# A fused attention and Fourier-mixing kernel: the first head pair folded too, 32 more score scans in the front, and the loop's cross products spread over 32 more steps

## The chip, the cores and the metric

The kernel runs on one core of one Trainium2 chip. The metric is device time in microseconds of one execution; the median of the runs shown is taken. In this text TensorE is PE in the profile's rows (its weight loads PEld), VectorE is DVE, ScalarE is ACT, GpSimd is POOL, and SyncE, which issues most of the transfers, is SP.

## The reference

For one sequence of 2048 rows of width 512, a gate mixes two results:

```python
g = sigmoid((x * gate_w).sum(-1, keepdims=True))
qkv = x @ wqkv                                   # 32 heads of width 16
a = softmax(q @ k^T * 16**-0.5) @ v @ wo         # per head, then the output projection
b = dft_seq_re @ (x @ dft_hid_re^T) - dft_seq_im @ (x @ dft_hid_im^T)
out = g * a + (1 - g) * b
```

All of it is in single precision. The weights of the attention are 64 times as large as is usual, so that the softmax needs the maximum of each row of scores subtracted.

## The kernel before, in words

The 32 heads are worked as 16 pairs. A float32 operand is split into a high and a low part, and a product is three matmuls (high by high, high by low, low by high). Most matmuls have at most 64 rows of the array and run as two side by side, each 512 columns wide; such a side-by-side couple is called a **slot** below (`halves_of` issues one, line 204).

**Scans.** Before a pair's exponentials can be taken, the maximum of each row of its scores must be known. A *scan* (there are 64 for a pair, 1024 in all) computes 128 query rows against 512 keys for both heads of the pair, one slot of TensorE work. A *plain* scan (`scan`, line 154) leaves the maximum to one VectorE reduction over 1024 numbers. A *folded* scan (`scan_folded`, line 173) works on key blocks two and two: the even block holds the difference of the keys of two blocks, ScalarE takes its positive part into the tile `fold` (line 177), and VectorE adds the odd block's scores and takes the maximum (line 179). That needs *key differences* in DRAM (`kf_d`), next to the plain keys (`k_d`).

**The front**, the first 655 us, is a sequence of products written out by hand: projections of q and k (`project_t`, 32 tiles of 12 slots), of v and the two hidden-side Fourier products (`project_s`, 48 tiles of 12 slots), and then most of the sequence-side Fourier product (22 tiles of 48 slots). Each product slot calls `beside`, which puts a scan between them at the spacing that `scan_at` sets (`PACE`, `SUMS`, `BESIDE`, `PART`, `SWAP`: so many product slots to a scan), until `FRONT` scans are done. Small steps are queued with `after(n, ...)`, n product slots ahead; each engine takes its steps in the order in which they were issued. In the kernel before, the 64 scans of pair 0 are plain and the other 644 of the front are folded. The key differences of pairs 4 to 7 are made when their keys are projected (`difference`), those of pairs 0 to 3 and 8 to 11 later, by `fold_keys`, which reads keys back from DRAM.

**The loop** has 512 steps, 32 for each pair. A step multiplies q by 128 keys for 1024 queries of both heads (line 229: one slot into a two-bank tile, `qk_both`, and one slot into two single banks, `qk_single`), takes the exponentials on ScalarE (line 253, 1024 columns, tile `eb`; line 261, twice 512 columns, tiles `e`), and multiplies the exponentials of an earlier step by v (line 775, tile `pvb`). Up to step `MIX` a step also has one plain scan. From `MIX` on the scans are done, and each step takes one piece of `fill`: first 32 steps of the sequence-side Fourier product (`spectral`), then the seven *cross products* (`crosses`, 14 tiles of 24 slots, as 8 pieces of 3 slots each), and from step `OUT` on the output projection (`mix_heads`, 9 slots a tile, in two pieces of 4 and 5 slots or four pieces of 2, 2, 2 and 3, and then `mix_some`). From `MIX` on the products with v of two steps are issued together in the even step:

```python
for _ in range(min(len(pend), 1) if step < MIX else 0 if step % 2 else 2):
    done = flush()
```

An even step's piece of `fill` is issued ahead of its products of q and k, an odd step's behind them, so the two pieces of an odd step and the even step behind it stand next to each other on TensorE. `qk_both` has one two-bank tile, which the next step needs again; `qk_single` takes its two banks out of three in turn (`bank`), so that one of the two was used in the step before.

Of the kernel before, what the change touches and what calls it, by code (L numbers as in the profile page):

```python
# [18 lines left out]
P = 128  # L19
# [17 lines left out]
SAVED = 2 * CROSS  # L37
# [5 lines left out]
PART_PAIR, END_PAIR = PARTS  # L43
SEQ = [(p, i) for p in EARLY for i in range(SCANS)]
SEQ += [(p, i) for p, n in PARTS.items() for i in range(n)]
SEQ += [(p, i) for p in (PART_PAIR, 12, 13, 14, 15, END_PAIR) for i in range(PARTS.get(p, 0), SCANS)]
ROWS = {SCANS * n + (20 if n else 40): p for n, p in enumerate(EARLY[1:])}
ROWS.update({SCANS * len(EARLY) - 60: PART_PAIR, SCANS * len(EARLY) - 34: END_PAIR})
NWARM = 20
MIX = TOTAL - FRONT + 1  # L50
OUT = MIX + NB * LATER - SAVED
HALVED = MIX + NB * (LATER - CROSS)
SLOW = 3
# [13 lines left out]
def build(tc, xT, wqkv, wo, wrT, wiT, cr, ci, ct, gate, out):  # L67
    nc = tc.nc
    with ExitStack() as ctx:
# [112 lines left out]
        def shift(p, copy=nc.vector.tensor_copy, sub=nc.vector.tensor_sub):  # L182
# [10 lines left out]
            of = mx[p].rearrange("p j b c -> p (j b) c")[:, :, 0:2 if p in EARLY[1:] else 4]  # L193
# [76 lines left out]
        with ExitStack() as pf:  # L270
# [36 lines left out]
            def beside():  # L307
# [6 lines left out]
                while seen[0] < FRONT and pace[1] >= 1.0:  # L314
                    pace[1] -= 1.0
                    n = seen[0]
                    if n == FOLDED.start:
# [20 lines left out]
            def behind(n):  # L338
                if n in FOLDED:
                    scan_folded(n, 1, *beds)  # L340
                    return n
# [49 lines left out]
            def begin_folds():  # L391
# [4 lines left out]
                scan_at(BESIDE)  # L396

            with ExitStack() as px:
# [28 lines left out]
                def fold_keys(f, g):  # L427
# [3 lines left out]
                    parts = [(a, b)]  # L431
                    if f:
                        for i, v in enumerate((a, b)):
                            nc.sync.dma_start(v, ks_d[f][:, (c + i) * 512:(c + i + 1) * 512])
                    else:

                        parts.append([rp.tile([P, 512], F32, tag="raw", name="fl") for _ in range(2)])
                        for n in range(2):
                            for i in range(2):
                                nc.sync.dma_start(parts[n][i], k_d[f][:, n, (c + i) * 512:(c + i + 1) * 512])  # L440
                        nc.sync.dma_start(kf_d[f][:, :, (c + 1) * 512:(c + 2) * 512],
                                          k_d[f][:, :, (c + 1) * 512:(c + 2) * 512])
# [6 lines left out]
                    wait = 0 if f else 26  # L449
                    after(14 + wait // 2, nc.gpsimd.tensor_sub, a, a, b)  # L450
                    if wait:
                        after(33, nc.gpsimd.tensor_sub, parts[1][0], *parts[1])
                        after(39, nc.gpsimd.tensor_add, a, a, parts[1][0])
                    after(wait + 22, nc.scalar.copy, hi, a)
                    after(wait + 24, nc.gpsimd.tensor_sub, lo, a, hi.bitcast(F32))
                    after(wait + 28, store, 0, hi)
                    after(wait + 31, store, 1, lo)
# [3 lines left out]
                def difference(f, c, s):  # L461
# [6 lines left out]
                    hi = ep.tile([P, 512], F32R, tag="gb", name="dh", bufs=1)  # L468
                    lo = a.bitcast(F32R)
# [10 lines left out]
                def project_t(w, dst, f, c, ps=None):  # L480
# [5 lines left out]
                    s = ep.tile([P, 512], F32, tag="ty", name="s", bufs=3)  # L486
# [3 lines left out]
                    on_vector = pace[0] in (None, SUMS)  # L490
                    if on_vector:
                        after(5, nc.vector.tensor_add, s, ps[1], tx)
                    else:
                        after(3, nc.scalar.copy, s, ps[1])
                        after(5, nc.gpsimd.tensor_add, s, s, tx)
                    late = 0 if on_vector else 6

                    def store(i, v):
                        nc.sync.dma_start(dst[f][:, i, c * 512:(c + 1) * 512], v.bitcast(F32))
                        if folded and f and c % 2:  # L500
# [6 lines left out]
                    after(9 + late, nc.scalar.copy, hi, s)  # L507
                    after(10 + late + late // 3, nc.gpsimd.tensor_sub, lo, s, hi.bitcast(F32))
                    after(14 + late, store, 0, hi)
                    after(20 + late, store, 1, lo)  # L510
# [72 lines left out]
                order += [(w, dst, 0, c) for c in range(1, NC) for w, dst in ((wq, q_d), (wk, k_d))]  # L583
# [22 lines left out]

                for t in range(NB):
# [22 lines left out]
                for n, wait in enumerate((18, 78, 138, 202)):  # L630
                    after(wait, fold_keys, 2 * (n // 2), n % 2)
# [20 lines left out]
            with ExitStack() as py:  # L652
# [36 lines left out]
                for n, (ph, t, u) in enumerate(coef):  # L689
# [6 lines left out]
                    if n == len(coef) - 2 * NU:  # L696
# [632 lines left out]
```

## Time and profile before

| what | value |
|---|---|
| median of 3 runs (lowest, highest) | 1714.47 us (1714.12 to 1715.61) |
| the profiled execution's own time | 1715.43 us |
| its span in the profile | 1713.6 us |
| TensorE clock granted | 0.999 |
| busy: PE, PEld, DVE, ACT, POOL | 99%, 60%, 69%, 87%, 45% |
| first scan of the front; first exponentials of the loop | 58 us; 658.5 us |
| loop, first to last tile `eb` | 658.5 to 1695.9 us, 512 of them |

A row of a group of instructions has the source line, the engine, the operation, the tiles written and read, the shapes and a count, then busy time and the mean of one, then the idle time ahead of them and what ended it. A row of the timeline has its start, its length, and the instructions merged into it. Matmuls are pipelined and their ends are modelled, so that a busy TensorE says little by itself; counts of matmuls in a stretch and start times say more.

### The profile page before, as it was taken

How to read it: one execution, taken by the hardware profiler on the slowest of the kernel's cores; microseconds unless marked ns; L12 is line 12 of the kernel's file. 1: busy time of each engine (PE TensorE's matmuls, PEld its weight loads, DVE VectorE, ACT ScalarE, POOL GpSimd, SP SyncE). 2: the span in 40 equal slices, each digit the busy share in tenths (PEclk: the TensorE clock that was granted, in tenths of full speed). 3: DMA queues.
4: the chain of work that ended last, by engine and by line, in shares of the span. 5: the costliest groups of instructions: out<-in, count | busy, mean ns of one | idle time of the engine just before them, and what ended most of it. 6: DMA issues, size and time to landing. Idle time of an engine off the chain costs nothing.

```text
span 1713.6 us, 36496 instructions
## 1 busy us (share of the span) xinstructions
PE 1700.1 (99%) x13560; PEld 1033.2 (60%) x13560; DVE 1189.9 (69%) x2179; ACT 1496.6 (87%) x2472; POOL 764.1 (45%) x909
## 2 busy tenths in 40 slices
PE   9999999999999999999999999999999999999998
PEld 6888888989888895333333333333345555555554
DVE  5798888889899996666666676666642455654343
ACT  6447889888888888999999999999998988888876
POOL 3583335755555762433535455353422333334222
PEclk9999999999999999999999999999999999999999
DMA  7783457533337665356544445453436465576733
GB/s 255 237 286 86 149 153 224 155 107 108 112 106 199 176 132 109 89 128 149 138 112 113 121 114 135 100 124 85 95 73 144 133 148 148 141 160 168 192 93 126
DMA packets 148962, 240.97 MB, mean 141 GB/s; under 512 B 50048, under 2 KB 60784, under 8 KB 142192
## 3 DMA queue, kind: packets, MB, share of 16 engines
q1 hardware_dynamic: 133520, 217.27, 47.5%
q0 software_dynamic: 14688, 20.33, 5.0%
q8 instruction: 106, 1.74, 0.5%
q10 hardware_dynamic: 576, 1.05, 0.2%
q14 instruction: 72, 0.59, 0.1%
HBM read 158.34 MB, written 81.01 MB: 140 GB/s over the span
## 4 chain that ended last, share of the span: by engine, by line
PE 95%; issue 1%; POOL 1%; DMA 1%; DVE 1%; ACT 0%; SPq 0%; DVEq 0%; POOLq 0%; ACTq 0%
PE pvb L775 29%; PE xy L204 24%; PE s L229 19%; PE s L173 9%; PE s L204 9%; PE s L154 5%; POOL el L297 1%; DMA raws<-wqkv 0%; DMA qs<-q_d 0%; DVE y L890 0%; DVE fold L179 0%; ACT fold L177 0%; DVE s L297 0%; SPq L543 0%; SPq L542 0%
## 5 line engine op out<-in xcount | busy, mean ns | idle before, releaser
L253 ACT ACTIVATE eb<-s 128x1024 f32<-128x1024 f32 x512 | 582.0, 1137 | 59.6 <-PE s L229 59.5
L261 ACT ACTIVATE e<-s 128x512 f32<-128x512 f32 x1022 | 612.3, 715 | 0.0
L156 DVE TENSOR_REDUCE mx<-s 128x2 f32<-128x1024 f32 x380 | 461.0, 1224 | 197.5 <-PE s L154 197.3
L775 PE MATMUL pvb<-eb,va 128*17 128x512 f32 x2052 | 514.6, 597 | 0.0
L775 PE MATMUL pvb<-e,va 128*17 128x512 f32 x2044 | 513.6, 597 | 0.0
L179 DVE CUSTOM_DVE_ANT_0 fold<-s,fold 128x512 f32<-128x512 f32 x644 | 433.2, 690 | 57.3 <-PE s L173 29.9
L177 ACT ACTIVATE fold<-s 128x512 f32<-128x512 f32 x644 | 381.4, 603 | 76.8 <-PE s L173 58.9
L229 PEld LDWEIGHTS s<-qs,ks 50*128 50x128 f32 x2048 | 215.4, 185 | 361.4 <-ACT eb L253 269.4
L229 PE MATMUL s<-qs,ks 50*128 50x512 f32 x2048 | 424.3, 435 | 0.0
L204 PE MATMUL xy<-b,c 64*128 64x512 f32 x2448 | 394.7, 392 | 0.2 <-ACT c L352 0.2
L173 PE MATMUL s<-ks,qs 48*128 48x512 f32 x1288 | 306.1, 403 | 1.7 <-DVE mx L179 0.9
L204 PEld LDWEIGHTS xy<-b,c 64*128 64x128 f32 x2448 | 285.7, 187 | 16.9 <-issue 1.0
L173 PEld LDWEIGHTS s<-ks,qs 48*128 48x128 f32 x1288 | 167.1, 184 | 40.4 <-DVE mx L179 10.7
L775 PEld LDWEIGHTS pvb<-eb,va 128*17 128x17 f32 x2052 | 70.0, 96 | 188.1 <-issue 178.5
L154 PE MATMUL s<-ks,qs 48*128 48x512 f32 x760 | 158.5, 394 | 0.9 <-DMA qs<-q_d 0.9
L204 PE MATMUL s<-b,b 64*128 64x512 f32 x1050 | 136.3, 391 | 0.0
L794 POOL DMA_DIRECT2D r_d<-lc x31 | 18.0, 580 | 260.6 <-DVE lc L793 212.9
L204 PE MATMUL xy<-w,b 64*128 64x512 f32 x768 | 114.8, 392 | 0.0
L204 PEld LDWEIGHTS s<-b,b 64*128 64x128 f32 x1050 | 100.3, 185 | 23.4 <-issue 1.0
L787 POOL DMA_DIRECT2D lc<-ob x124 | 63.0, 515 | 114.4 <-DVE ob L784 109.6
L384 POOL TENSOR_TENSOR c<-craw,c 128x512 fp32r<-128x512 f32 x84 | 110.2, 1312 | 6.7
L796 POOL DMA_DIRECT2D rb<-r_d x124 | 60.5, 494 | 110.6 <-DMA r_d<-lc 104.7
(148 smaller groups left out, 1567.3 us busy)
## 6 DMA issues: line engine op xcount, KB each, us to landing
qs<-q_d SPq DMA_DIRECT2D x68, 256.0 KB
craw<-cr SPq DMA_DIRECT2D x60, 256.0 KB
craw<-ct SPq DMA_DIRECT2D x48, 256.0 KB
ks<-k_d SPq DMA_DIRECT2D x46, 256.0 KB
kept_None<-sum SPq DMA_DIRECT2D x40, 256.0 KB
craw<-kept_None SPq DMA_DIRECT2D x40, 256.0 KB
qs<-q_d SPq DMA_DIRECT2D x68, 128.0 KB
craw<-ci SPq DMA_DIRECT2D x32, 256.0 KB
```

The costliest lines, as they stand in the source:

```text
L154: nc.tensor.matmul(ps[:, j, :], qs[b:b + 48, qb * P:(qb + 1) * P], ks[b:b + 48, c * 512:(c + 1) * 512], start=True, stop=True)
L156: nc.vector.tensor_reduce(mx[p][:, :, qb, c], ps, axis=AX.X, op=ALU.max)
L173: nc.tensor.matmul(ps, qs[b:b + 48, qb * P:(qb + 1) * P], ks[b:b + 48, c * 512:(c + 1) * 512], start=True, stop=True)
L177: nc.scalar.activation(fold[j], ps, AF.Relu)
L179: nc.vector.tensor_tensor_reduce(out=fold[j], in0=ps, in1=fold[j], scale=1.0, scalar=-3.0e38, op0=ALU.add, op1=ALU.max, accum_out=mx[p][:, ...
L204: nc.tensor.matmul(ps[j], lhs[r], rhs[r], start=first, stop=last)
L229: nc.tensor.matmul(pss[j], ks[b:b + 50, kb * P:(kb + 1) * P], qs[b:b + 50, q0:q0 + 512], start=True, stop=True)
L253: nc.scalar.activation(e, ps, AF.Exp, scale=SCALE)
L261: nc.scalar.activation(e[j], pss[j], AF.Exp, scale=SCALE)
L384: sub(lo, raw, hi.bitcast(F32))
L775: nc.tensor.matmul(pvb[r:r + VC, :], va[:, kb, 2 * p + j, :], es[c][j], start=kb == 0, stop=kb == NB - 1, tile_position=(0, r))
L787: nc.gpsimd.dma_start(lc[32 * n:32 * n + 32, :], ob[r + DH:r + VC, :].rearrange("p (s e) -> p s e", e=16))
```

## The change

- Pair 0 is folded like the others. Its key differences, and those of pairs 1 to 3, are made in the prologue by `difference`, from the sums while they are still in SBUF; the projections of k are issued ahead of those of q in the first row group for that. `fold_keys` now serves pairs 8 to 11 and 12 to 15.
- The front has 740 scans in place of 708, all folded: the pairs in order 0 to 10 whole, 16 of pair 12 and 20 of pair 11. The spacing is narrower in the projections of q and k (2.95 and 3.6 for 3.9 and 5.2 product slots to a scan) and a little narrower in the last part (2.11 for 2.15). The sum of the two halves of a projection is always taken on VectorE now.
- `MIX` goes from step 317 to 285. The cross products of a tile are cut into 10 pieces (3, 2, 2, 3, 2, 2, 3, 2, 2, 3 slots) in place of 8 pieces of 3, so they take 140 steps in place of 112. `OUT` goes from 461 to 457, and five tiles of the output projection in place of three are cut into four pieces.

```diff
-FRONT = 564 + 16 * LATER - SAVED
-FOLDED = range(SCANS, FRONT)
-PACE, SUMS, BESIDE, PART, SWAP = 3.9, 5.2, 2.72, 2.15, 2.97
-EARLY = [0, 4, 5, 6, 7, 1, 2, 3, 8, 9]
-PARTS = {10: 20, 11: FRONT - SCANS * len(EARLY) - 20}
+EARLY = range(11)
+PARTS = {12: 16, 11: 20}
+FRONT = SCANS * len(EARLY) + sum(PARTS.values())
+PACE, SUMS, BESIDE, PART, SWAP = 2.95, 3.6, 2.72, 2.11, 2.97
...
-OUT = MIX + NB * LATER - SAVED
 HALVED = MIX + NB * (LATER - CROSS)
-SLOW = 3
+STEPS = [3, 2, 2, 3, 2, 2, 3, 2, 2, 3]
+TURN = 2 * len(STEPS)
+OUT = HALVED + 7 * TURN
+SLOW = 5
...
-                scanned[p], loads = row_loads(p, nc.sync, kf_d if p else k_d)
+                scanned[p], loads = row_loads(p, nc.sync, kf_d)
...
-                    if n not in FOLDED:
-                        scan(n, s1())
-                        done = n
-                    else:
-                        scan_folded(n, 0, *beds)
-                        done = behind(n - 1)
+                    scan_folded(n, 0, *beds)
+                    done = behind(n - 1)
...
-                    hi = ep.tile([P, 512], F32R, tag="gb", name="dh", bufs=1)
-                    lo = a.bitcast(F32R)
+                    hi = (ep.tile([P, 512], F32R, tag="gb", name="dh", bufs=1) if f else
+                          rp.tile([P, 512], F32R, tag="raw", name="dh"))
+                    lo = b.bitcast(F32R)
...
-                    on_vector = pace[0] in (None, SUMS)
-                    if on_vector:
-                        after(5, nc.vector.tensor_add, s, ps[1], tx)
-                    else:
-                        after(3, nc.scalar.copy, s, ps[1])
-                        after(5, nc.gpsimd.tensor_add, s, s, tx)
+                    after(5, nc.vector.tensor_add, s, ps[1], tx)
...
-                    if folded and f == 1:
+                    if folded and f < 2:
                         difference(f, c, s)
-                    if folded and f == 2:
+                    if folded and f > 1:
                         after(10, nc.sync.dma_start, ks_d[f][:, c * 512:(c + 1) * 512], s)
...
-                order += [(w, dst, 0, c) for c in range(1, NC) for w, dst in ((wq, q_d), (wk, k_d))]
+                order += [(w, dst, 0, c) for c in range(1, NC) for w, dst in ((wk, k_d), (wq, q_d))]
...
-                    after(wait, fold_keys, 2 * (n // 2), n % 2)
+                    after(wait, fold_keys, 2 + n // 2, n % 2)
...
                     for f in range(2):
                         ps = pair_banks()
+                        done = 0
                         for u in range(8):
...
                                 halves_of((ps[:, 0, :], ps[:, 1, :]), left[a][:, q], right[b],
                                           u == 0 and i == 0, u == 7 and i == 2)
-                            if u < 7:
-                                yield
+                                done += 1
+                                if done in [sum(STEPS[:k]) for k in range(1, len(STEPS))]:
+                                    yield
```

**The loop's cross products, on TensorE.** Before, between the products of q and k of an odd step and those of the even step behind it (`s<-qs,ks`: one row of x2 for the two-bank tile, two rows for the single banks) there stand six slots of the cross product, three of each step:

```order
L229 MATMUL s_20824<-qs,ks 128x512 x2
L229 MATMUL s_20828<-qs,ks 128x512
L229 MATMUL s_20829<-qs,ks 128x512
L204 MATMUL s_20834<-b_20671,b_20624 128x512 x2
L204 MATMUL s_20834<-b_20672,b_20624 128x512 x2
L204 MATMUL s_20834<-b_20671,b_20625 128x512 x2
L204 MATMUL s_20834<-b_20701,b_20624 128x512 x2
L204 MATMUL s_20834<-b_20702,b_20624 128x512 x2
L204 MATMUL s_20834<-b_20701,b_20625 128x512 x2
L229 MATMUL s_20853<-qs,ks 128x512 x2
```

Now there are five at such a place (and four at every fifth):

```order
L229 MATMUL s_21047<-qs,ks 128x512 x2
L229 MATMUL s_21051<-qs,ks 128x512
L229 MATMUL s_21052<-qs,ks 128x512
L204 MATMUL s_20922<-b_20931,b_20909 128x512 x2
L204 MATMUL s_20922<-b_20957,b_20908 128x512 x2
L204 MATMUL s_20922<-b_20958,b_20908 128x512 x2
L204 MATMUL s_20922<-b_20957,b_20909 128x512 x2
L204 MATMUL s_20922<-b_20977,b_20908 128x512 x2
L229 MATMUL s_21067<-qs,ks 128x512 x2
```

The products with q and k and with v that stand around them are the same and stand in the same places; only the number of slots between them is smaller, and there are more such places.

**The first scans, on TensorE.** Before, the first scans of the front stand in the projections of q (`xy<-b,w`) and each is a plain scan, both heads together, with four product slots to one:

```order
L204 MATMUL xy<-b_227,w_236 128x512 x2
L154 MATMUL s_959<-ks,qs 128x512 x2
L204 MATMUL xy<-b_229,w_235 128x512 x2
L204 MATMUL xy<-b_230,w_235 128x512 x2
L204 MATMUL xy<-b_229,w_236 128x512 x2
L204 MATMUL xy<-b_231,w_235 128x512 x2
L154 MATMUL s_973<-ks,qs 128x512 x2
```

Now the first head of a scan stands beside the second head of the one before, with three product slots to one:

```order
L204 MATMUL xy<-b_228,w_235 128x512 x2
L173 MATMUL s<-ks,qs 128x512
L204 MATMUL xy<-b_227,w_236 128x512 x2
L204 MATMUL xy<-b_229,w_235 128x512 x2
L204 MATMUL xy<-b_230,w_235 128x512 x2
L173 MATMUL s<-ks,qs 128x512 x2
L204 MATMUL xy<-b_229,w_236 128x512 x2
```

A scan comes one product slot sooner, and needs the second head's rows at the second scan, not the first.

**ScalarE in the projections of k.** Before, a tile's steps there are the copy of one half of the sum (`tx`), sometimes that of the other (`s`), and the high part (`eh`, `dh` for the difference), beside the split of a weight (`w`); the plain scans need nothing of ScalarE:

```order
L489 COPY tx<-xy 128x512
L352 CAST w_1140<-wraw 128x512
L297 CAST eh<-s 128x512
L489 COPY tx<-xy 128x512
L297 COPY s<-xy 128x512
L297 CAST dh<-s 128x512
```

Now the positive parts of the folded scans (`fold`) stand between them:

```order
L471 COPY tx<-xy 128x512
L177 ACTIVATE fold<-s 128x512 x2
L347 CAST w_1220<-wraw 128x512
L177 ACTIVATE fold<-s 128x512
L297 CAST eh<-s 128x512
L177 ACTIVATE fold<-s 128x512 x2
```

Four positive parts are added to a tile of twelve product slots, and the copy `s` is gone.

More of the change, by code (lines that the diff above doesn't have):

```diff
@@ L430, in fold_keys @@
                     c = 2 * g
[L431 to L434, printed above, removed]
-                    else:
[L437 to L442, printed above, removed]
+                    for i, v in enumerate((a, b)):
+                        nc.sync.dma_start(v, ks_d[f][:, (c + i) * 512:(c + i + 1) * 512])
                     hi = ep.tile([P, 512], F32R, tag="gb", name="fh", bufs=1)
@@ L447, in store @@
                         nc.sync.dma_start(kf_d[f][:, i, c * 512:(c + 1) * 512], v.bitcast(F32))
[L449 to L457, printed above, removed]
+                    after(14, nc.gpsimd.tensor_sub, a, a, b)
+                    after(22, nc.scalar.copy, hi, a)
+                    after(24, nc.gpsimd.tensor_sub, lo, a, hi.bitcast(F32))
+                    after(28, store, 0, hi)
+                    after(31, store, 1, lo)
                 kept = []
@@ L485, in project_t @@
                     folded = dst is k_d
-                    s = ep.tile([P, 512], F32, tag="ty", name="s", bufs=3)
+                    s = (rp.tile([P, 512], F32, tag="raw", name="s") if folded and not f else
+                         ep.tile([P, 512], F32, tag="ty", name="s", bufs=3))
                     hi = ep.tile([P, 512], F32R, tag="eh", name="eh", bufs=3)
```

41 lines of the change are left out of this document (19 added, 22 removed).

## The prediction

> **What bounds the kernel now.** I read the windows by stage first, with the number of instructions in each, since busy time says little of TensorE. Columns: stretch, its length, then busy time and count of PE, PEld, DVE, ACT and POOL, granted clock, DMA share and GB/s. The rows are the projections ahead of the first scan, those with plain scans, the sequence-side product with folded scans, the loop with scans, and the loop with cross products:
>
> ```profile
> 38.00:52.00 14.00, 14.00 (x126) 11.63 (x124) 7.30 (x9) 7.47 (x15) 6.05 (x6) 1.00 0.78 238
> 60.00:115.00 55.00, 55.00 (x473) 46.59 (x472) 54.46 (x50) 25.72 (x48) 41.91 (x34) 1.00 0.66 237
> 400.00:520.00 120.00, 119.99 (x1011) 108.10 (x1010) 108.67 (x327) 101.39 (x179) 65.12 (x68) 1.00 0.38 111
> 700.00:1200.00 500.00, 500.00 (x3696) 191.76 (x3696) 338.80 (x314) 500.00 (x793) 228.11 (x315) 1.00 0.49 119
> 1320.00:1560.00 240.00, 240.00 (x1978) 127.14 (x1976) 133.63 (x205) 213.81 (x331) 92.01 (x126) 1.00 0.58 145
> ```
>
> The front is a stream of slots on TensorE: 126 matmuls, 63 slots, in 14.00 us are 0.222 us a slot, and with scans between them 1011 matmuls fill 120 us (0.237 us). In the loop with scans ScalarE is busy for all of 500.00 us and bounds it. With cross products ScalarE has 26 us idle in 240, and PE is "busy" throughout: whether it is full is the question on which the forecast turns. The loop's step comes from the first and last start of `eb` in those two windows (minimum, median, maximum duration first):
>
> ```profile
> L253 ACT ACTIVATE eb<-s x265: 1095/1229/1254, 698.8 to 1199.6; 128x1024 f32<-128x1024 f32 x133
> L253 ACT ACTIVATE eb<-s x111: 1025/1032/1046, 1319.2 to 1559.8; 128x1024 f32<-128x1024 f32 x111
> ```
>
> 264 steps in 500.8 us: a scan step takes **1.897 us**. 110 steps in 240.6 us: a cross step takes **2.187 us**, with three slots.
>
> So what does a scan-free step with fewer than three slots take? The trace has some: the first tiles of the output projection are cut into 2, 2, 2 and 3. ScalarE's timeline there (start, length):
>
> ```profile
> 1572.94 1.03 ACT L253 ACTIVATE eb<-s 128x1024 f32<-128x1024 f32 x1 [0.47 <-PE s L229]
> 1574.82 1.04 ACT L253 ACTIVATE eb<-s 128x1024 f32<-128x1024 f32 x1
> ...
> 1577.32 1.03 ACT L253 ACTIVATE eb<-s 128x1024 f32<-128x1024 f32 x1 [0.47 <-PE s L229]
> 1578.24 1.08 ACT L261 ACTIVATE e<-s 128x512 f32<-128x512 f32 x2
> 1579.19 1.04 ACT L253 ACTIVATE eb<-s 128x1024 f32<-128x1024 f32 x1
> ...
> 1581.68 1.03 ACT L253 ACTIVATE eb<-s 128x1024 f32<-128x1024 f32 x1 [0.47 <-PE s L229]
> ...
> 1583.56 1.04 ACT L253 ACTIVATE eb<-s 128x1024 f32<-128x1024 f32 x1
> ...
> 1586.06 1.03 ACT L253 ACTIVATE eb<-s 128x1024 f32<-128x1024 f32 x1 [0.48 <-PE s L229]
> ...
> 1588.62 1.02 ACT L253 ACTIVATE eb<-s 128x1024 f32<-128x1024 f32 x1 [0.56 <-PE s L229]
> ...
> 1591.13 1.03 ACT L253 ACTIVATE eb<-s 128x1024 f32<-128x1024 f32 x1 [0.51 <-PE s L229]
> ```
>
> Two steps with the last six slots of a cross product take 1577.32 - 1572.94 = 4.38 us. The next two have four slots: 4.36 us. The next two have five: 4.38 us. Only with nine does it grow: 5.07 us. **Below six slots the pair of steps does not get shorter.** The weight loads and matmuls of the four-slot pair, and of a six-slot one for comparison, show why:
>
> ```profile
> 1402.34 1.54 PE L204 MATMUL s<-b,b 64*128 64x512 f32 x12
> ...
> 1577.34 1.09 PE L204 MATMUL s<-b,b 64*128 64x512 f32 x8
> 1578.39 0.29 PEld L229 LDWEIGHTS s<-qs,ks 50*128 50x128 f32 x3 [0.39 <-ACT eb L253]
> 1578.88 0.18 PEld L229 LDWEIGHTS s<-qs,ks 50*128 50x128 f32 x1 [0.19 <-ACT e L261]
> ```
>
> After eight matmuls the even step's products of q and k wait for ScalarE: `qk_both` until `eb` has left its two-bank tile (0.39 us), and the second half of `qk_single` until the first `e` of the step before has left its bank (0.19 us). So a pair of steps is a cycle through both engines: products of q and k, exponentials `eb` and `e` (1577.32 to 1579.19, 1.87 us), the second bank, then the products with v of two steps and the next products of q and k (1579.19 to 1581.68, 2.49 us). Six slots just fit into the first part of it.
>
> **The loop, part by part.**
>
> *32 scan steps go*: 32 x 1.897 = -60.7 us.
>
> *28 cross steps come* (140 for 112). The pieces make pairs of five, five, four, five and five slots, which by the rows above take 4.36 to 4.38 us, not less: 28 x 2.187 = +61.2 us. The slots themselves, 336 in all, are the same and stay hidden in the cycle.
>
> *Two more tiles of the output projection are cut in four*: each takes two pairs (4.36 + 4.38) for one of 5.07: 2 x 3.67 = +7.3 us.
>
> Together **+7.8 us**: 32 steps have changed from 1.897 us to the longer cycle, and nothing is saved by their shorter filling. Loads, splits of operands and gathers of the cross products keep their distance of some steps to their use, and DVE has 106 of 240 us free there: nothing. Steps in all (512), the order of the pairs and the tail stay.
>
> **The front: 32 more scans.** Of the matmuls in two of the windows above, those of line 204 are products:
>
> ```profile
> 60.00:115.00 55.00, 53.17 (x381) 41.32 (x382) 1.00 0.66 237
> 400.00:520.00 120.00, 115.51 (x689) 82.87 (x690) 1.00 0.38 111
> ```
>
> From 400 to 520 us 344.5 product slots at 0.222 take 76.6 us, and the 161 scans the other 43.4: **0.270 us a scan**. From 60 to 115 us the 46 plain scans take 55.0 - 42.3 = 12.7 us, 0.275 each, so folding pair 0 changes nothing on TensorE. TensorE is the limit in the whole front, so 32 scans cost 32 x 0.270 = +8.6 us; bounds are a bare product slot (0.222, +7.1 us) and 0.275 (+8.8 us). The Trainium skill, "TensorE: Matmul & The Clock Gate", section "Back-to-back issue gap", gives 512 columns / 2.4 GHz + 2.5 ns, 216 ns; an estimate from that page is 32 x 0.216 = 6.9 us. The trace's bare slot is 3% above it and a scan 25%, and the measurement decides.
>
> What else could wait in the front? These are the waits between 40 and 660 us that touch scans or the key differences (total, times, longest):
>
> ```profile
> PEld s L173 <- DVE mx L179: 10.7, 40, 0.9
> PEld s L173 <- ACT fold L177: 6.0, 16, 0.8
> ACT dh L297 <- POOL s L297: 2.3, 2, 1.2
> PE s L154 <- DMA qs<-q_d: 0.9, 1, 0.9
> ```
>
> *The first scan* waited 0.9 us for the rows of its second head. Now the second head comes one scan later (gain up to 0.9), but the rows come from `kf_d`, whose differences pass GpSimd and ScalarE and are stored late in the prologue, and SyncE issues the stores ahead of the row loads (loss perhaps as much). I take -0.5 us.
>
> *The projections of k* get four positive parts a tile on ScalarE. Mean durations by groups, and then a stretch of ScalarE's timeline in the scanning loop, where it is back to back:
>
> ```profile
> L177 ACT ACTIVATE fold<-s 128x512 f32<-128x512 f32 x644 | 381.4, 603 | 76.8 <-PE s L173 58.9 <-DVE mx L179 3.6
> L297 ACT CAST eh<-s 128x512 fp32r<-128x512 f32 x32 | 19.9, 621 | 18.5 <-DVE s L297 16.2 <-DMA q_d<-eh 2.3
> L489 ACT COPY tx<-xy 128x512 f32<-128x512 f32 x28 | 16.4, 585 | 27.7 <-PE xy L204 15.8 <-POOL s L297 11.8
> L179 DVE CUSTOM_DVE_ANT_0 fold<-s,fold 128x512 f32<-128x512 f32 x644 | 433.2, 690 | 57.3 <-PE s L173 29.9 <-ACT fold L177 11.8 <-issue 0.8
> L156 DVE TENSOR_REDUCE mx<-s 128x2 f32<-128x1024 f32 x380 | 461.0, 1224 | 197.5 <-PE s L154 197.3
> ```
>
> ```profile
> 900.81 1.30 ACT L261 ACTIVATE e<-s 128x512 f32<-128x512 f32 x2
> 901.78 1.25 ACT L253 ACTIVATE eb<-s 128x1024 f32<-128x1024 f32 x1
> ```
>
> A tile of 12 products and 4 scans takes TensorE 12 x 0.222 + 4 x 0.270 = 3.74 us. ScalarE's durations in it are 4 x 0.603 + 0.585 + 0.621 = 3.62 us, and 4.24 in a tile that also splits a weight (taken as another 0.62). But durations overlap: the two `e` are over only after 1.30 us, yet the `eb` behind them starts after 901.78 - 900.81 = 0.97, so a 512-column operation takes some 0.49 us in a row, and a tile of six or seven 2.9 to 3.4 us. Upper bound: 0.5 us too much in four tiles, 2 us; lower bound none. VectorE has 4 x 0.690 = 2.8 us and a sum, less than the 3 x 1.224 = 3.7 us of plain reductions of before, which kept it 99% busy (54.46 of 55 us) with TensorE at 0.275 a scan. The `dh` steps hold ScalarE's queue for 1.2 us each, with positive parts now queued behind, and behind these TensorE's next scan into the same bank; two such cost at most 2.4 us. Nearest is the row of 400 to 520 us, ScalarE 84% busy and TensorE not held: I take +0.5 us for all of this, 0 to 4.4.
>
> Front: 8.6 - 0.5 + 0.5 = **+8.6 us**. The key work that `fold_keys` no longer does for pairs 0 to 3 was on GpSimd and SyncE, beside the products, and so was what it now does for 12 to 15: nothing.
>
> **Sum.** 7.8 + 8.6 = +16.4 us. The profiled execution took 1715.43 us, 1.8 over its span of 1713.6; with the change the span would be 1730.0 and the time 1731.8. The median of the runs is 0.96 below the profiled one, so I predict **1730.9 us**. A measurement of this kernel can tell about 0.2%, 3.4 us.
>
> **The rivals.**
>
> *The spread steps are full on TensorE* (6%; faster). If a cross step were bound by its slots, a slot would be worth (5.07 - 4.38) / 3 = 0.23 us, a step without filling 2.187 - 3 x 0.23 = 1.50 us, and as the slots are only moved, the loop would change by 32 x (1.50 - 1.897) = -12.7 us. With +8.6 in the front that is -4.1: 1710.4 us. It decides if a pair with four or five slots falls below 4.1 us. For it: the slots from six to nine do cost 0.23 each. Against it: the 4.36 and 4.38 us of the same trace; but these are two pairs, next to another stage, so some chance is left. The Trainium skill, "Perfetto Trace Analysis", section "Optimization Strategy", says that where the most-contended engine changes from regime to regime, interleaving the regimes may help, which is what spreading the cross products among the exponentials does. By that rule the pairs with four and five slots would be shorter, and in this trace they are not.
>
> *The front hides the scans* (4%; slower by less). If TensorE had idle time there, only the loop's +7.8 would be left: 1722.3 us. Against it: 0.237 us a slot over 120 us.
>
> *The prologue jams* (9%; slower by more). ScalarE, waiting for GpSimd at `dh` and shared with the positive parts, or SyncE's queue, with stores of differences ahead of row loads, holds TensorE's scans by 5 to 12 us: 1736 to 1743 us. For it: the tiles with a weight split are near ScalarE's limit by durations. Against it: the same engine at 84% further on holds nothing.
>
> *The forecast* has the other 81%.
>
> **Range and chances.** The forecast's own ends: low, front 7.1 - 0.9 and loop 7.8, +14.0, 1728.5; high, front 8.8 + 0.9 + 4.4 and loop 7.8 plus 0.5 for pairs a little longer, +22.4, 1736.9. I take 1727 to 1738, which holds the forecast and the lesser half of the jam. The first rival ends just beyond the bound: of its 6%, I count 0.04 as faster by over 0.2% and 0.02, its mild form, as within 0.2%. Slower by over 0.2% is the rest, 0.94.
>
> **What would show it.** In the trace after: cross steps at 2.187 us a step over 140 steps, with weight loads of line 229 waiting for `eb` and `e` in each pair; scan steps at 1.897 as before; the first `eb` some 8.6 us later, near 667 us. I am wrong if `eb` starts of two cross steps lie clearly under 4.3 us apart, if the first `eb` is not later, or if waits for `fold` in the first 130 us come to more than 5 us.

## The result, and the profile after

The changed kernel takes 1735.53 us (median of 4 runs, 1735.17 to 1735.89) against 1714.87 us of the kernel before on the same chip (4 runs, 1714.12 to 1715.61): a ratio of **1.0121** [1.0103, 1.0138], 20.7 us slower. Predicted were 1730.9 us, 1727 to 1738. The profiled execution took 1735.44 us, its span is 1733.6 us, 20.0 more than before's.

Where the 20 us lie is read from the starts of the loop's 512 tiles `eb`, one a step. Their groups in the two profiles, before's row first (minimum, median, maximum duration, then first and last start):

```profile
L253 ACT ACTIVATE eb<-s x512: 1023/1138/1254, 658.5 to 1695.9; 128x1024 f32<-128x1024 f32 x171
```

```profile
L253 ACT ACTIVATE eb<-s x512: 1023/1092/1256, 669.4 to 1715.9; 128x1024 f32<-128x1024 f32 x171
```

The front ends 11.0 us later (669.45 for 658.49, with one more digit), and the loop takes the other 9.0 us. Counting the starts of `eb` off at `MIX`, `MIX` + 32 and `OUT` splits the loop further (us; "of the scans" runs from step 2):

| stage | before | after | difference | predicted |
|---|---|---|---|---|
| front, to the first `eb` | 658.49 | 669.45 | +10.96 | +8.6 |
| steps of the scans (315; 283) | 597.36 | 537.33 | -60.03 | -60.7 |
| sequence-side product (32) | 70.19 | 70.21 | +0.02 | 0 |
| cross products (112; 140) | 244.98 | 306.33 | +61.35 | +61.2 |
| output projection and last pairs | 118.59 | 126.30 | +7.71 | +7.3 |
| tail | 17.74 | 17.68 | -0.06 | 0 |

These are the windows of the changed kernel that answer to those of before (columns as there): the sequence-side product in the front, the loop with scans, and the loop with cross products, which are later by the front's difference and longer.

```profile
400.00:520.00 120.00, 120.00 (x1012) 107.34 (x1010) 109.46 (x329) 101.53 (x180) 64.45 (x68) 1.00 0.42 120
720.00:1200.00 480.00, 479.60 (x3542) 180.04 (x3534) 329.88 (x303) 479.71 (x760) 225.15 (x311) 1.00 0.49 124
1320.00:1580.00 260.00, 260.00 (x2000) 122.30 (x1999) 117.18 (x186) 231.80 (x358) 94.78 (x131) 1.00 0.50 127
```

From 400 to 520 us TensorE issues 1012 matmuls, where before it issued 1011: the same work at the same rate. The loop with scans is bound by ScalarE as before (479.71 of 480 us). With cross products there are now 7.69 matmuls a microsecond (2000 / 260), before 8.24 (1978 / 240), and PE is shown busy throughout in both, so its busy share says nothing of how full it is. The starts of `eb` and the waits of the weight loads do. For the last window, the group of `eb`, and that of the weight loads of line 229 with what ended their waits (us, times):

```profile
L253 ACT ACTIVATE eb<-s x119: 1024/1043/1048, 1320.2 to 1578.4; 128x1024 f32<-128x1024 f32 x119
```

```profile
L229 PEld LDWEIGHTS s<-qs,ks x473: 182/183/190, 1319.9 to 1578.1; 50*128 50x128 f32 x158
...
  ACT e L261: 60.4, 115
  ACT eb L253: 9.5, 43
```

and before's own weight loads there, with six slots in every pair:

```profile
L229 PEld LDWEIGHTS s<-qs,ks x440: 182/184/188, 1320.4 to 1559.4; 50*128 50x128 f32 x147
...
  ACT e L261: 46.8, 55
```

118 steps in 258.2 us are **2.188 us a step**; it was 2.187 with a quarter more filling (six slots a pair, now 4.8 in the mean). Before, these loads stood still once in each of 55 pairs, for 0.85 us behind the products with v (the row puts it down to `e`), and never for `eb`. That stop of 0.85 us is still there in each pair, as long as it was; new are waits for `eb`, 43 in 59 pairs of steps and up to 0.39 us long, and some 55 more for `e`, up to 0.19 us, as in before's four-slot pair. They come to about 0.33 us a pair, so the time of the 1.2 slots that went has become waiting. ScalarE's timeline over three pairs (the even steps; the first pair has four slots, the other two five):

```profile
1467.11 1.03 ACT L253 ACTIVATE eb<-s 128x1024 f32<-128x1024 f32 x1 [0.47 <-PE s L229]
...
1471.48 1.03 ACT L253 ACTIVATE eb<-s 128x1024 f32<-128x1024 f32 x1 [0.47 <-PE s L229]
...
1475.85 1.03 ACT L253 ACTIVATE eb<-s 128x1024 f32<-128x1024 f32 x1 [0.47 <-PE s L229]
...
1480.22 1.03 ACT L253 ACTIVATE eb<-s 128x1024 f32<-128x1024 f32 x1 [0.48 <-PE s L229]
```

Each pair takes 4.37 us, whether it has five slots or four.

**Where the front lost more than predicted.** TensorE's timeline in the prologue, first of the kernel before, then of the changed one: from the hidden-side products on, the rows with a wait ahead of them, of before also the row at the place where the changed kernel waits, and of the changed kernel the first folded scan.

```profile
10.79 3.04 PE L204 MATMUL xy<-b,c 64*128 64x512 f32 x24 [0.22 <-ACT c L352]
...
27.27 3.33 PE L204 MATMUL xy<-b,w 64*128 64x512 f32 x24
```

```profile
11.57 3.04 PE L204 MATMUL xy<-b,c 64*128 64x512 f32 x24 [0.55 <-ACT c L347]
...
28.44 0.51 PE L204 MATMUL xy<-b,c 64*128 64x512 f32 x2 [0.23 <-ACT b L347]
29.83 0.96 PE L204 MATMUL xy<-b,c 64*128 64x512 f32 x6 [0.88 <-DVE b L348]
31.52 2.53 PE L204 MATMUL xy<-b,c 64*128 64x512 f32 x16 [0.73 <-DVE b L348]
...
60.73 0.39 PE L173 MATMUL s<-ks,qs 48*128 48x512 f32 x1
```

Between 28 and 32 us TensorE waits three times for parts `b` of x, which ScalarE rounds and VectorE completes; before, there is no such wait. Counted by weight loads, the 160th starts at 24.43 us (23.65 before) and the 200th at 31.63 us (28.19): 0.8 us are lost ahead of this place and **2.7 us** in it. ScalarE's and GpSimd's timelines of the changed kernel there:

```profile
23.97 0.62 ACT L297 CAST eh<-s 128x512 fp32r<-128x512 f32 x1 [1.16 <-DVE s L297]
24.50 0.58 ACT L471 COPY tx<-s 128x512 f32<-128x512 f32 x1
27.25 0.62 ACT L297 CAST dh<-s 128x512 fp32r<-128x512 f32 x1 [2.17 <-POOL s L297]
27.77 0.61 ACT L347 CAST b<-raws 128x512 fp32r<-128x512 f32 x1
...
28.82 0.61 ACT L347 CAST b<-raws 128x512 fp32r<-128x512 f32 x1
```

```profile
24.67 1.30 POOL L297 TENSOR_TENSOR el<-s,eh 128x512 fp32r<-128x512 f32 x1 [2.53 <-ACT eh L297]
25.92 1.30 POOL L297 TENSOR_TENSOR s<-s 128x512 f32<-128x512 f32 x1
```

The high part of the key difference (`dh`) stands at the head of ScalarE's queue and waits 2.17 us for GpSimd, which has first the low part `el` and then the difference itself to make, 1.30 us each. The splits of x (`b`) for the next row group stand behind it, and TensorE waits for them.

### The profile page after: what moved, and what is told of

Same layout as the page of the kernel before. It is cut to its first block, busy times and chain, and to the rows that moved or that the text cites. A ratio compares the mean times of both kernels' runs of the same rounds, so it can differ in the third digit from the quotient of the medians.

```text
span 1733.6 us, 36853 instructions
## 1 busy us (share of the span) xinstructions
PE 1718.4 (99%) x13560; PEld 1034.1 (60%) x13560; DVE 1149.3 (66%) x2290; ACT 1540.4 (89%) x2554; POOL 744.8 (43%) x893
## 4 chain that ended last, share of the span: by engine, by line
PE 95%; DMA 2%; DVE 1%; SPq 0%; issue 0%; POOL 0%; ACT 0%; DVEq 0%; POOLq 0%; ACTq 0%
PE pvb L752 28%; PE xy L204 25%; PE s L229 19%; PE s L173 11%; PE s L204 8%; PE s L154 4%; DMA raws<-wqkv 0%; DMA q_d<-eh 0%; DMA raws<-xT 0%; DVE fold L179 0%; PE s L549 0%; DVE y L867 0%; SPq L780 0%; DMA b<-o_d 0%; DVE b L348 0%
## 5 line engine op out<-in xcount | busy, mean ns | idle before, releaser
L253 ACT ACTIVATE eb<-s 128x1024 f32<-128x1024 f32 x512 | 571.7, 1117 | 67.0 <-PE s L229 66.9
L261 ACT ACTIVATE e<-s 128x512 f32<-128x512 f32 x1022 | 602.1, 695 | 0.0
L179 DVE CUSTOM_DVE_ANT_0 fold<-s,fold 128x512 f32<-128x512 f32 x740 | 497.8, 690 | 67.7 <-PE s L173 37.2
L177 ACT ACTIVATE fold<-s 128x512 f32<-128x512 f32 x740 | 437.2, 603 | 84.9 <-PE s L173 65.8
L156 DVE TENSOR_REDUCE mx<-s 128x2 f32<-128x1024 f32 x284 | 348.0, 1225 | 171.7 <-PE s L154 171.6
L229 PE MATMUL s<-qs,ks 50*128 50x512 f32 x2048 | 435.3, 439 | 0.0
L229 PEld LDWEIGHTS s<-qs,ks 50*128 50x128 f32 x2048 | 210.0, 184 | 371.8 <-ACT eb L253 252.1
L204 PE MATMUL xy<-b,c 64*128 64x512 f32 x2496 | 405.8, 392 | 2.5 <-DVE b L348 1.6
L173 PE MATMUL s<-ks,qs 48*128 48x512 f32 x1480 | 356.7, 403 | 1.8 <-DVE mx L179 1.3
L173 PEld LDWEIGHTS s<-ks,qs 48*128 48x128 f32 x1480 | 194.4, 184 | 46.0 <-DVE mx L179 10.8
L154 PE MATMUL s<-ks,qs 48*128 48x512 f32 x568 | 114.9, 395 | 0.1
L773 POOL DMA_DIRECT2D rb<-r_d x124 | 60.5, 495 | 106.4 <-DMA r_d<-lc 101.0
```

Source lines behind the costliest of these rows:

```text
L154: nc.tensor.matmul(ps[:, j, :], qs[b:b + 48, qb * P:(qb + 1) * P], ks[b:b + 48, c * 512:(c + 1) * 512], start=True, stop=True)
L156: nc.vector.tensor_reduce(mx[p][:, :, qb, c], ps, axis=AX.X, op=ALU.max)
L173: nc.tensor.matmul(ps, qs[b:b + 48, qb * P:(qb + 1) * P], ks[b:b + 48, c * 512:(c + 1) * 512], start=True, stop=True)
L177: nc.scalar.activation(fold[j], ps, AF.Relu)
L179: nc.vector.tensor_tensor_reduce(out=fold[j], in0=ps, in1=fold[j], scale=1.0, scalar=-3.0e38, op0=ALU.add, op1=ALU.max, accum_out=mx[p][:, ...
L204: nc.tensor.matmul(ps[j], lhs[r], rhs[r], start=first, stop=last)
```

## Experiments

Two questions were open: what holds a pair of cross steps at 4.37 us (theory A: the cycle through q,k products, exponentials and products with v; theory B: TensorE's own slots, or ScalarE alone), and what the front pays for. Ratios are to the kernel before on the same chip.

**One third of the cross products' slots left out, in the kernel before.**

```diff
-    for i, (a, b) in enumerate(((0, 0), (0, 1), (1, 0))):
+    for i, (a, b) in enumerate(((0, 0), (0, 1))):
```

> The kernel before, with the third product of each step of the cross products (low by high) left out: two slots to a piece for three, so 112 of 336 cross slots are gone and each pair of cross steps has four. Theory A (a pair of scan-free steps is a cycle through ScalarE and TensorE of 4.37 us, in which up to six slots are hidden): nothing changes, 1714.9 us, cross steps 2.187 us. Rival B (cross steps are full on TensorE, 0.23 us a slot): 112 x 0.23 = 25.8 us less, 1689 us, cross steps 1.96 us.

Measured: 1714.91 us, 1.0005 [0.9996, 1.0015]. TensorE lost 112 slots and no time was gained. The group of `eb` with cross products, and of TensorE's timeline one pair, matmuls first and then the weight loads:

```profile
L253 ACT ACTIVATE eb<-s x111: 1025/1044/1049, 1319.3 to 1559.8; 128x1024 f32<-128x1024 f32 x111
```

```profile
1400.52 1.09 PE L204 MATMUL s<-b,b 64*128 64x512 f32 x8
...
1401.57 0.29 PEld L229 LDWEIGHTS s<-qs,ks 50*128 50x128 f32 x3 [0.40 <-ACT eb L253]
1402.05 0.18 PEld L229 LDWEIGHTS s<-qs,ks 50*128 50x128 f32 x1 [0.19 <-ACT e L261]
```

110 steps in 240.5 us are 2.186 us, with four slots in every pair; the waits for `eb` (0.40 us) and `e` (0.19 us) are those that the prediction read from one pair of before. Below six slots the pair gets no shorter, whatever stands in it, and the rival of full spread steps falls.

**The first of the two products with v ahead of the even step's single-bank products**, so that the cycle gets shorter; in the changed kernel and in the one before, the same edit:

```diff
                 if step > 2:
+                    if step >= MIX and step % 2 == 0:
+                        flush()
                     es.append(qk2(p, h, kb, 1))
...
-                for _ in range(min(len(pend), 1) if step < MIX else 0 if step % 2 else 2):
+                for _ in range(min(len(pend), 1) if step < MIX else 0 if step % 2 else 1):
```

> The changed kernel, with one edit in the loop: from MIX on, the first of the two products with v of an even step is issued ahead of qk_single, not behind it, so that TensorE has work while the second bank is still being read. Theory A: the wait for the first e goes out of the cycle; pairs with five slots take about 4.14 us and those with four 3.9 to 4.05, the cross products lose some 18 us and the output projection 3: 1712 to 1715 us. Rival B (full on TensorE): nothing, 1735.5. Rival A2 (the cycle runs through the two-bank tile of qk_both alone): little, over 1730.

> The kernel before, with the same edit of the order of the products with v. Theory A: pairs with six slots have TensorE full already (4.36 us of work in 4.37), so the cross steps stay at 2.18 us, and only the three tiles of the output projection cut in four gain 0.7 us each: about 1712.5 us. Rival B: nothing, 1714.9.

Measured: 1752.54 us, 1.0221 [1.0206, 1.0237], from the changed kernel, and 1741.56 us, 1.0159 [1.0142, 1.0176], from before. Both are slower, and both expectations (1712 to 1715 and 1712.5 us) missed. The group of `eb` with cross products in the edited kernel of before, and a pair of steps on TensorE:

```profile
L253 ACT ACTIVATE eb<-s x103: 1024/1030/1047, 1319.1 to 1557.8; 128x1024 f32<-128x1024 f32 x103
```

```profile
1401.61 1.54 PE L204 MATMUL s<-b,b 64*128 64x512 f32 x12
1402.99 0.40 PE L229 MATMUL s<-qs,ks 50*128 50x512 f32 x2
1403.32 0.61 PE L775 MATMUL pvb<-eb,va 128*17 128x512 f32 x2
...
1404.31 0.50 PE L229 MATMUL s<-qs,ks 50*128 50x512 f32 x2
1404.74 0.61 PE L775 MATMUL pvb<-eb,va 128*17 128x512 f32 x2
```

A step takes 238.7 / 102 = 2.340 us, a pair 4.68 in place of 4.37. The matmuls are the same and none waits for ScalarE; what is new is that TensorE goes from products of q and k to those with v and back twice in a pair in place of once. With six slots, where TensorE is the limit, that one change more takes **0.31 us** a pair (4.68 - 4.37). With fewer slots a pair takes less. ScalarE's timeline of the edited form of the changed kernel (even steps), and the weight loads of the cross product (line 204) and those that wait for `eb`, over a pair of five slots and then one of four:

```profile
1405.35 1.03 ACT L253 ACTIVATE eb<-s 128x1024 f32<-128x1024 f32 x1 [0.30 <-PE s L229]
...
1409.80 1.03 ACT L253 ACTIVATE eb<-s 128x1024 f32<-128x1024 f32 x1 [0.30 <-PE s L229]
...
1414.25 1.03 ACT L253 ACTIVATE eb<-s 128x1024 f32<-128x1024 f32 x1 [0.30 <-PE s L229]
```

```profile
1405.15 1.12 PEld L204 LDWEIGHTS s<-b,b 64*128 64x128 f32 x10
1406.43 0.19 PEld L229 LDWEIGHTS s<-qs,ks 50*128 50x128 f32 x2 [0.16 <-ACT eb L253]
...
1409.60 0.89 PEld L204 LDWEIGHTS s<-b,b 64*128 64x128 f32 x8
1410.88 0.19 PEld L229 LDWEIGHTS s<-qs,ks 50*128 50x128 f32 x2 [0.39 <-ACT eb L253]
```

Both pairs take 4.45 us. The short wait for `e` is gone, as meant, but the wait for `eb` is not, and it is longer with four slots (0.39 us) than with five (0.16). So below six slots the edited pair is still a cycle whose length does not depend on its slots, 0.08 us longer than 4.37: the change of products that the edit adds stands in the cycle too, and costs more there than the wait it removes. The expectations had put that change at nothing.

**The exponentials shortened**: from `MIX` on the first of a step's two single-bank exponentials takes 256 of its 512 columns; in the changed kernel and in before, the same edit.

```diff
-                nc.scalar.activation(e[j], pss[j], AF.Exp, scale=SCALE)
+                c = slice(0, n if j else 512)
+                nc.scalar.activation(e[j][:, c], pss[j][:, c], AF.Exp, scale=SCALE)
```

> The changed kernel, with the first of a step's two single-bank exponentials (the one whose bank the next step needs) taken over 256 of its 512 columns from MIX on; the other 256 are left out. It shortens that exponential by 0.21 us. Theory A (the cycle of a pair runs through it, with slack on TensorE below six slots): pairs with four and five slots fall by about 0.2 us, 80 pairs in all, 17 us: about 1718 us. Rival: if the pair is held elsewhere (the products with v, or slots), nothing: 1735.5.

> The kernel before, with the same exponential cut to 256 columns from MIX on. Theory A: pairs with six slots have TensorE full at 4.36 us, so they gain 0 to 0.02 us each, and only the six pairs with four or five slots gain 0.2: 1712 to 1713.5 us. Rival (ScalarE alone bounds the scan-free steps): 0.2 us for each of some 97 pairs, 1695 us.

Measured: 1717.85 us, 1.0023 [1.0014, 1.0033], and 1711.67 us, 0.9986 [0.9977, 0.9995]. From the same cut the changed kernel gains 17.7 us and the kernel before 2.6, 0.3 us past the lower end of what was expected. The groups of `eb` with cross products, changed kernel first:

```profile
L253 ACT ACTIVATE eb<-s x126: 1023/1029/1046, 1321.3 to 1581.5; 128x1024 f32<-128x1024 f32 x126
```

```profile
L253 ACT ACTIVATE eb<-s x111: 1023/1025/1032, 1319.2 to 1559.3; 128x1024 f32<-128x1024 f32 x111
```

The steps with five and four slots go from 2.188 to 2.082 us (260.2 / 125), those with six only to 2.183 (240.1 / 110). So ScalarE's part of the cycle holds the changed kernel's pairs. In the kernel before, TensorE's own work in a pair with six slots is as long as the cycle: that kernel sits at the knee, where neither thinner filling nor a faster cycle gains. ScalarE alone as the limit would have taken before to 1695 us, and falls.

**The front alone**: the changed front, with the loop of before (its 32 steps with scans repeat scans).

```diff
-TOTAL = SCANS * NP
+TOTAL = SCANS * NP + 32
...
-STEPS = [3, 2, 2, 3, 2, 2, 3, 2, 2, 3]
+STEPS = [3] * 8
...
-SLOW = 5
+SLOW = 3
```

> The changed kernel's front with the loop of before: MIX, the pieces of the cross products and of the output projection as before, and the 32 scan steps kept, which repeat scans of the last pair. By the split of the two traces (front +11.0 us, loop +9.0) this is 1725 us if the parts add up; by my prediction's front, 1722.7. If the front's loss were made up by the loop, or came with it, 1714 or 1735.

Measured: 1728.21 us, 1.0081 [1.0066, 1.0096], 13.9 us over before, 3 more than expected. By the stages the front ends at 670.17 us and the loop is 1.1 us longer than before's. So the front is the larger part of the change's cost, and the part that I had put too low.

**The high part of the difference 8 product slots later**, in the changed kernel, for the pairs whose differences are made in the prologue:

```diff
-                    after(16, nc.scalar.copy, hi, a)
-                    after(17, nc.gpsimd.tensor_sub, lo, a, hi.bitcast(F32))
-                    after(22, store, 0, hi)
-                    after(25, store, 1, lo)
+                    late = 0 if f else 8
+                    after(16 + late, nc.scalar.copy, hi, a)
+                    after(17 + late, nc.gpsimd.tensor_sub, lo, a, hi.bitcast(F32))
+                    after(22 + late, store, 0, hi)
+                    after(25 + late, store, 1, lo)
```

> The changed kernel, with the high part of the differences of pairs 0 to 3 (dh), its low part and its stores queued 8 product slots later in the prologue. Theory P (ScalarE stood 2.2 us at dh for GpSimd's difference, the splits of x behind it came late, and TensorE waited for them): the 1.9 us of waits for b between 28 and 34 us go, 1733 to 1734 us. Rival (the prologue is held by the transfers of x): nothing, 1735.5.

Measured: 1733.58 us, 1.0113 [1.0098, 1.0128], 1.95 us less than the changed kernel, as expected, or 1.2 us less if each is set against the kernel before on its own chip. ScalarE's timeline at the place, and then TensorE's longest wait there:

```profile
24.93 0.62 ACT L347 CAST b<-raws 128x512 fp32r<-128x512 f32 x1
...
27.67 0.62 ACT L297 CAST dh<-s 128x512 fp32r<-128x512 f32 x1 [0.69 <-POOL s L297]
```

```profile
31.17 0.96 PE L204 MATMUL xy<-b,c 64*128 64x512 f32 x6 [1.32 <-DVE b L348]
```

The split of x that stood behind `dh` at 27.77 us now starts at 24.93, and the first scan's weight load comes at 59.5 us in place of 60.5. The first `eb` comes at 668.15 us; in four profiles with `dh` where it was it comes at 669.45 to 670.25. The wait at the head of ScalarE's queue is thus shown as a cause. It is not all of it: 1.8 of the 2.7 us are still lost in the stretch, now later in the same tile.

**The change turned round**: 32 scans fewer in the front, and the cross products in pieces of four slots (84 steps); then 28 fewer, with the output projection cut as before.

```diff
-FRONT = 564 + 16 * LATER - SAVED
+FRONT = 564 + 16 * LATER - SAVED - 32
...
+TURN = 12
...
-                            if u < 7:
-                                yield
+                                done += 1
+                                if done % 4 == 0 and done < 24:
+                                    yield
```

> The opposite of the change, made from the kernel before: 32 scans fewer in the front, MIX 32 steps later, cross products in six pieces of four slots (84 steps), one tile of the output projection cut in four in place of three; the pair with the last folded scans comes second among the loop's scans, since its maxima are needed there. Theory A (a knee at six slots a pair): front -8, scan steps +60.7, cross steps 42 x 4.84 - 245 = -41.8, output projection -7.3: about +3.5, 1717.6 us. Rival C (every scan moved to the front loses what it lost in the change, 0.65 us, whichever way): -20, 1694 us.

> The opposite of the change again, with 28 scans fewer in the front, so that the rows of the next pair are loaded in the part of a pair's steps in which buffers are free (with 32 fewer the loop stood four times some 12 us for those rows). Cross products in six pieces of four slots, output projection as before. Theory A (knee at six slots): front -7.5, 28 scan steps +53.1, cross steps 42 x 4.82 - 245 = -42.6: +3.0, 1717 us. Rival C (every scan moved to the front costs 0.65 us, whichever way): -18, 1696 us.

Measured: 1769.68 us, 1.0322 [1.0305, 1.0340], and 1729.51 us, 1.0078 [1.0063, 1.0094]; expected were about 1717 for both. The totals are spoiled by a wait that I had not seen coming: from the timelines of TensorE, first the kernel with 32 scans fewer at one of four such places, then the one with 28 fewer at one of three:

```profile
834.47 0.76 PE L155 MATMUL s<-ks,qs 48*128 48x512 f32 x1 [5.77 <-DMA qs<-q_d]
839.23 0.76 PE L155 MATMUL s<-ks,qs 48*128 48x512 f32 x1 [4.00 <-DMA qs<-q_d]
```

```profile
983.51 0.50 PE L155 MATMUL s<-ks,qs 48*128 48x512 f32 x2 [3.35 <-DVE mx L157]
```

With another order of scans the first kernel's rows of q (`qs`) came late, and the whole loop stood; the second's wait is put down to VectorE's maximum, and its cause was not taken apart. Stage by stage the parts can still be read. The 347 and 343 steps of scans take 710.55 and 662.05 us; at before's 1.896 us a step they would take 658.1 and 650.5, so the waits and what came behind them cost 52 and 12 us. The group of `eb` with cross products in the second kernel:

```profile
L254 ACT ACTIVATE eb<-s x84: 1023/1027/1046, 1384.2 to 1583.7; 128x1024 f32<-128x1024 f32 x84
```

199.5 / 83 = 2.404 us a step, 4.81 a pair of eight slots: two slots more than the knee cost 0.44 us, 0.22 each. The 84 steps take 202.4 us, 42.5 less than before's 112. Without the 12 us the second kernel would be near 1718 us, an estimate from this one profile; its four runs spread from 1723.21 to 1730.12 us. That the change turned round is itself slower than before is therefore likely, but not shown.

**Six scans back into the loop**, the output projection uncut:

```diff
-FRONT = 564 + 16 * LATER - SAVED
+FRONT = 564 + 16 * LATER - SAVED - 6
...
-SLOW = 3
+SLOW = 0
-TURNED = 476
+TURNED = 482
```

> A candidate to beat the kernel before: six scans go back from the front to the loop, and no tile of the output projection is cut in four (the turned rows are loaded six steps later, since the cross products end six steps later). Theory A: the three tiles lose a pair with four or five slots each and keep one with nine, 3 x -3.67 = -11.0; six scan steps +11.4; front 6 x -0.27 = -1.6: -1.2, 1713 us where before is 1714.2. If pairs below six slots were shorter than 4.37: slower than before, by 0.7 or more.

Measured: 1713.85 us, 0.9996 [0.9987, 1.0005]: no difference from before can be told. The scans' stage grows by 11.5 us and the output's shrinks by 10.4. No version that was run is clearly faster than before, except before with its exponential cut short, which leaves work out.

## Why the prediction was right, and where it was off

**The loop: right in mechanism and size.** Predicted +7.8 us, measured +9.0. The step of 2.187 us for pairs of five and four slots came out at 2.188, over 140 steps. The chain of waits behind it is shown by taking slots away (nothing changes) and by shortening an exponential (17.7 us in the changed kernel, 2.6 in before). What the change does there is to turn 32 steps of 1.897 us, bound by ScalarE, into steps of 2.188 us, bound by a cycle through both engines: moving filling out of a pair that is already at the knee saves nothing. The missing 1.2 us are scan steps that are 0.002 us longer (1.8987 for 1.8964, 283 of them: 0.65 us) and 0.4 us in the output projection. They need not come from the thinner pieces: behind the changed front before's own loop was 1.1 us longer too (0.4 us in its scan steps, 0.7 in its output projection). Why is open.

**The front: right in its main term, too low by the prologue.** The term "I take +0.5 us for all of this" is the step that failed. Its mechanism, `dh` at the head of ScalarE's queue while GpSimd makes the difference, I had priced from the stage with scans (two waits of 1.2 us), with positive parts and scans queued behind it. It struck in the prologue, where the change makes four pairs' differences for the first time: there the splits of x are behind it, and TensorE loses 2.7 us, of which the later `dh` gives back 0.9 in the same stretch and 1.2 to 1.95 in the whole time.

The 32 scans themselves are near their price. From the first scan (57.5 and 60.7 us) to the first `eb` it is 601.0 us before and 608.7 after. The profiled execution of before lost some 1.5 us just behind its first scan, where it waited for rows; three other profiles of the same front take 599.4 to 599.7 us there, and four of the changed front 608.5 to 609.5. That is +9.5 us, against 8.6 for the scans at 0.270 and 0.6 for pair 0, whose folded scans cost a little more than its plain ones. The latter is read from the window from 66 to 126 us of the changed kernel, all of TensorE and then line 204 alone:

```profile
66.00:126.00 60.00, 59.98 (x506) 50.53 (x504) 51.12 (x141) 52.52 (x100) 30.55 (x25) 1.00 0.79 279
```

```profile
66.00:126.00 60.00, 57.36 (x382) 42.98 (x380) 1.00 0.79 279
```

191 product slots at 0.222 are 42.4 us; the 62 scans take the other 17.6, 0.284 each, for 0.275 of the plain ones: 64 x 0.009 = 0.6 us. "Folding pair 0 changes nothing on TensorE" was wrong by that. The wait at the first scan, for which I took -0.5 us, is one execution's; where the same front was profiled again it was not there, so it was no term. With 3.3 to 3.6 us lost ahead of the first scan, the front costs 13.0 us between the means of those profiles (656.8 and 669.9 us to the first `eb`), and 11.0 against the one that I had; 20.7 us between the medians lies between the two sums (20.0 and 22).

**The rivals.** Full spread steps (1710.4 us): falls with the left-out slots. A front that hides the scans (1722.3 us): falls, by the front alone. The jammed prologue: its mechanism was the right one, at 2.7 us rather than 5 to 12, and at x rather than at the positive parts. It is the largest single part of the 4.6 us by which the result stands above the forecast, inside the range; the rest is in the smaller terms above.

**Left open.** 0.8 us are lost ahead of the first hidden-side product (11.57 for 10.79 us), in stretches that both kernels issue alike; of four other profiles of the changed front three show 11.47 to 11.52 and one 10.97, so it is not wholly steady. What holds the splits of x when `dh` comes later (1.8 us) was not taken apart either.

## What to carry to other kernels

Before work is spread thinner over a stage, look there for what a step costs with less of it: if the shortest steps in the trace are as long as the full ones, something other than the filling holds the stage, here a cycle between two engines, and filling saves time only when it is taken from above the place where the two limits meet. When work on an engine with a queue in order is moved to an earlier stage, price its wait by who stands behind it there, not by who stood behind it where it came from. A term read from one execution's wait deserves a second look at another profile of the same code.

## What had not been expected of the hardware

- Going once more from products of q and k (50 rows, two side by side) to products with v (128 rows, 17 columns) and back cost 0.31 us a pair of six slots (4.68 for 4.37), more than a whole slot (0.22 us), though no matmul was added.
- After a long wait TensorE is slow for some microseconds more. Windows of the kernel with 32 scans fewer, the first inside its wait of 4.00 us and the other two behind it:

```profile
836.00:839.00 3.00, 0.00 (x0) 0.00 (x0) 0.00 (x0) 0.00 (x0) 0.00 (x0) 0.50 0.89 186
839.00:843.00 4.00, 3.77 (x15) 1.37 (x17) 1.34 (x2) 1.08 (x2) 3.03 (x3) 0.50 0.73 280
843.00:847.00 4.00, 4.00 (x32) 1.41 (x30) 2.63 (x4) 3.98 (x7) 1.95 (x4) 1.00 0.36 92
```

The granted clock (the column behind the busy times) is 0.50 in the first two of these windows and 1.00 in the third, and 15 matmuls run from 839 to 843 us, 32 in the next 4 us. So a wait of that length costs more than itself. The Trainium skill, "TensorE: Matmul & The Clock Gate", section "What's actually happening", says that the clock falls to half after an idle window of about 3.4 us and comes back after a busy one; this trace agrees, with half the clock in a wait of 4.00 us and the full clock back 3.8 us after the work resumed at 839.23 us.
